# Converting float64 weights by a scaled copy and two bitwise VectorE operations

## The chip, the cores and the metric

The kernel runs on one core of a Trainium2 chip. The metric is the device time in microseconds (us), as the median of several runs; lower is better. TensorE (PE) does matrix products, VectorE (DVE), ScalarE (ACT) and GpSimd (POOL) do elementwise work, and SyncE (SP) issues most transfers.

## The reference, cut to what matters

```python
def reference(**kwargs):
    x = _attn_ref(q, k, v, mem_k, mem_v)          # chunked attention, 4 x 8 heads x 768 x 64
    x = x.transpose(0, 2, 1, 3).reshape(3072, 512)
    x = _moe_ref(x, w_gate, w1, w2)               # 8 experts, at most 384 tokens each
    return _moe2_ref(x, w1, w2, w3, w_out)        # (x@w1 * x@w2) @ w3 @ w_out

def _moe2_setup():
    n_tokens, d_model, d_ff = (3072, 512, 1024)
    return {'x': np.random.randn(n_tokens, d_model).astype(np.float32) * 0.3,
            'w1': np.random.randn(d_model, d_ff).astype(np.float32) * (1.0 / np.sqrt(d_model)),
            ...
```

The four weights of the last block arrive as float64: numpy promotes them when it multiplies by a float64 scalar. The kernel gets their raw bits, two 32-bit words for each number, and has to make float32 of them on the chip. Each is then split into a rounded high part and the rest (`hi`, `lo`), and products are made of three matmuls, so that they keep the accuracy of float32.

## The kernel before, in words

All instructions are written out by a planner in Python (`Plan.run`). Each piece of work is a generator that yields steps: engine letters ("P" TensorE, "V" VectorE, "A" ScalarE, "G" GpSimd, "D" a transfer), an estimated duration, the function that issues the instruction, and the time from which its inputs are there. The planner keeps a clock for each engine, takes the step that can start first, breaks ties by priority (a low number goes first), and so fixes the order of each engine's instructions. On the chip each engine works through its list in that order. A step marked "VG" goes to the one of VectorE and GpSimd that would end first, with 1.0 us (`BIAS`) added against VectorE.

The program has these stages, which overlap:

- Attention, up to about 97 us: 32 units (`unit`), each of score matmuls, softmax, transposes and value matmuls. TensorE, VectorE and ScalarE hand over to each other.
- Routing of expert 0 (`route(0)`), about 97 to 170 us: a search for a threshold, digit by digit. A digit is a compare over all tokens (L586, VectorE), counting matmuls (L651), a flag (L655), a summing matmul (L658) and small VectorE steps (L629, L644, L671). The stage ends with the tokens' indices (L773 to L791), then GpSimd gathers the tokens' rows (L829).
- In the same time `combine` multiplies w3 by w_out on TensorE (L503). It fills TensorE while the routing waits, and needs 24 converted tiles.
- The experts, from about 176 us: `first` (L489 to L491) and `second` over streamed weight blocks, `gate` (L927, L928, L935) with the 16 converted tiles of w1 and w2, `project` (L968, L969, L976), and the scatter. The routing of the next expert runs beside them. From about 246 us on the experts repeat.

The change touches `convert(n)`, which runs for 40 tiles of 128 x 512 numbers: n = 0 to 7 w_out (raw tiles `b`), n = 8 to 23 w3 (raw tiles `a`), n = 24 to 39 w1 and w2 (`a` and `b`). A tile needs two free places of 512 columns (`own`, `other`; mostly `cv`, also `x`). Its steps before:

- L448, ScalarE: the high word, read as float32, absolute value times 2^16, to `t`.
- L449, ScalarE: the top byte of the low word, to its top three bits as an integer, to `r`.
- L453 on GpSimd or L455 on VectorE: clamp, `t = max(t, 2.0)`.
- L458, VectorE: `t = (t << 3) | r`, bitwise, which gives the magnitude.
- n below 24 (`SIGNED`): L461, ScalarE, the sign of the high word to `r`; L462, GpSimd, `t = t * r`.
- n from 24: L465, VectorE: `t = (high & sign bit) | t`.
- L482, ScalarE: `hi`, the rounded copy. L399 on GpSimd or L401 on VectorE (`rest`): `lo = t - hi`.

The steps of `convert` have priority 70, those of a routing 50. L399 and L401 lie in the helper `rest`, which other stages use too.

Of the kernel before, what the change touches and what calls it, by code (L numbers as in the profile page):

```python
# [8 lines left out]
F32 = mybir.dt.float32  # L9
F32R = mybir.dt.float32r  # L10
BF16 = mybir.dt.bfloat16
I32 = mybir.dt.int32
U8 = mybir.dt.uint8
AF = mybir.ActivationFunctionType
OP = mybir.AluOpType
# [11 lines left out]
DM, DF, E = H * D, 1024, 8  # L27
CAP = N // E
NEG = -1.0e30
SIGNED = range(24)  # L30
STORE = 65
ABP = 61
ABN = 0
# [114 lines left out]
class Net:  # L148
# [289 lines left out]
    def convert(self, n):  # L438

        nc, V = self.nc, self.nc.vector  # L440
        t0 = yield from self.wait(("raw", n))
        places = [self.EARLY, self.CV] if n < 3 * FT else [self.CV]
        (own, tc, cv), (other, tr, r) = yield from Slots.pair(*places)
        tag, raw = self.raw.pop(n)
        t, ti = cv, cv.bitcast(I32)
        high = raw.rearrange("p (n w) -> p n w", w=2)[:, :, 1]
        byte = raw.bitcast(U8).rearrange("p (n w) -> p n w", w=8)[:, :, 3]
        e = yield ("A", 0.52, lambda: nc.scalar.activation(t, high.bitcast(F32), AF.Abs, scale=2.0 ** 16), max(t0, tc))  # L448
        er = yield ("A", 0.52, lambda: nc.scalar.activation(r.bitcast(I32), byte, AF.Copy, scale=1 / 32, bias=-31 / 64), max(t0, tr))  # L449

        def clamp(eng):
            if eng == "G":
                nc.gpsimd.tensor_scalar(t, t, 2.0, None, op0=OP.max)  # L453
            else:
                V.tensor_scalar(t, t, 2.0, None, op0=OP.max)  # L455

        e = yield ("VG", (0.34, 1.46), clamp, e)
        e = yield ("V", 0.60, lambda: V.scalar_tensor_tensor(  # L458
            ti, ti, 3, r.bitcast(I32), op0=OP.logical_shift_left, op1=OP.bitwise_or), max(e, er))
        if n in SIGNED:  # L460
            es = yield ("A", 0.52, lambda: nc.scalar.activation(r, high.bitcast(F32), AF.Sign), e)  # L461
            e = yield ("G", 1.23, lambda: nc.gpsimd.tensor_tensor(t, t, r, op=OP.mult), es)  # L462
            other.put(r, e)
        else:
            e = yield ("V", 0.60, lambda: V.scalar_tensor_tensor(  # L465
                ti, high, -2 ** 31, ti, op0=OP.bitwise_and, op1=OP.bitwise_or), e)
            other.put(r, e)
        self.at["read", n] = e
        if FT <= n < 3 * FT:
            m, i = divmod(n - FT, 2)  # L470
            if i == 0:
                ts, ws = yield from self.WS.get()
                self.wblk[m] = ts, ws, self.place(ws, [2, 2, 512], F32R)
            while m not in self.wblk:
                yield None
            ts, _, w = self.wblk[m]
            w = self.w[n] = w[:, i]
        else:
            ts, w = 0.0, self.place(tag, [2, 512], F32R)
            self.w[n] = w  # L480
        hi, lo = w[:, 0], w[:, 1]
        e = yield ("A", 0.52, lambda: nc.scalar.activation(hi, t, AF.Copy), max(e, ts))  # L482
        e = yield ("VG", (0.6, 1.23), lambda g: self.rest(hi, lo, t, g), e)
        own.put(cv, e)
        self.at["w", n] = e
# [622 lines left out]
```

## Time and profile before

| | |
|---|---|
| median of 3 runs | 923.13 us (922.63 to 924.12) |
| the profiled execution's own time | 923.5 us |
| its span in the trace | 921.7 us |
| mean granted TensorE clock | 0.983 of full speed |
| PE busy | 873.5 us (95%) |
| DVE busy | 613.2 us (67%) |
| ACT busy | 336.3 us (36%) |
| POOL busy | 203.4 us (22%) |

Busy times are those of the whole span. The stages differ much, so the rows further down are cut by stage. 1.8 us of the profiled execution's time lie outside its span.

### The profile page before, as it was taken

The numbers are of one execution on the slowest core, as the hardware profiler recorded it, in microseconds if no ns is written. First come the engines' busy times: TensorE is split into PE (matmuls) and PEld (weight loads), VectorE is DVE, ScalarE is ACT, GpSimd is POOL, SyncE is SP. The second block draws the span as 40 slices with busy tenths as digits, with TensorE's granted clock in tenths as the row PEclk, the third lists the DMA queues.
The fourth block names the chain that finished last, engine by engine and source line by source line (L and its number), as shares of the span: only waits on it lengthen the run. The fifth ranks groups of instructions, "written<-read, shape, count | busy, mean of one in ns | idle before, by whom it ended". The sixth has DMA issues, their size and how long they took to land.

```text
span 921.7 us, 16319 instructions
## 1 busy us (share of the span) xinstructions
PE 873.5 (95%) x6561; PEld 782.7 (85%) x6561; DVE 613.2 (67%) x1313; ACT 336.3 (36%) x593; POOL 203.4 (22%) x176
## 2 busy tenths in 40 slices
PE   6999877988998999999999999999999999999996
PEld 5777555887797998999899989979999999999995
DVE  7888799699875885789488767857764156213211
ACT  3778765466322331233223222321233134213211
POOL 3235677278642001101010101010110011001001
PEclk9999978997999999999999999999999999999999
DMA  8999880681061215025303601260141024002000
GB/s 298 403 343 390 302 292 7 215 309 55 16 186 44 80 69 154 35 70 134 88 35 114 174 3 57 94 175 1 55 152 46 1 81 162 10 1 103 1 1 34
DMA packets 36267, 110.36 MB, mean 120 GB/s; under 512 B 9440, under 2 KB 9952, under 8 KB 35552
## 3 DMA queue, kind: packets, MB, share of 16 engines
q1 hardware_dynamic: 32352, 96.74, 30.8%
q0 software_dynamic: 3840, 12.59, 4.3%
q8 instruction: 51, 0.84, 0.4%
q14 instruction: 24, 0.20, 0.1%
HBM read 96.24 MB, written 13.07 MB: 119 GB/s over the span
## 4 chain that ended last, share of the span: by engine, by line
PE 71%; DVE 17%; DMA 4%; issue 3%; ACT 2%; POOL 1%; SPq 0%; POOLq 0%; DVEq 0%; ACTq 0%
PE bank L927 9%; PE bank L935 9%; PE bank L928 8%; PE bank L489 7%; PE bank L490 7%; PE bank L491 7%; PE bank L976 5%; PE bank L968 5%; PE bank L969 4%; DVE kd L401 2%; PE bank L323 2%; DMA x<-xs,ix 2%; PE bank L340 2%; DVE ex L586 2%; PE bank L297 1%
## 5 line engine op out<-in xcount | busy, mean ns | idle before, releaser
L489 PE MATMUL bank<-x,kd 128*128 128x384 f32 x512 | 177.6, 347 | 0.1
L490 PE MATMUL bank<-x,kd 128*128 128x384 f32 x512 | 173.9, 340 | 1.3 <-DVE kd L401 1.3
L491 PE MATMUL bank<-x,kd 128*128 128x384 f32 x512 | 173.7, 339 | 0.0
L992 POOL DMA_INDIRECT out<-x,ix x24 | 23.4, 976 | 395.2 <-ACT x L987 392.2
L953 DVE TENSOR_TENSOR pt<-pt,bank 128x384 f32<-128x384 f32 x64 | 35.3, 552 | 111.5 <-PE bank L935 105.4
L490 PEld LDWEIGHTS bank<-x,kd 128*128 128x128 f32 x512 | 97.7, 191 | 3.0 <-DVE kd L401 2.3
L489 PEld LDWEIGHTS bank<-x,kd 128*128 128x128 f32 x512 | 97.7, 191 | 2.7 <-issue 1.6
L491 PEld LDWEIGHTS bank<-x,kd 128*128 128x128 f32 x512 | 97.4, 190 | 0.3 <-DVE x L401 0.3
L683 DVE TENSOR_SCALAR_CACHE_REDUCE ex<-cv,thf 128x1536 bf16<-128x1536 f32 x50 | 90.5, 1809 | 0.2
L927 PE MATMUL bank<-x,a 128*128 128x384 f32 x256 | 87.9, 343 | 0.0
L927 PE MATMUL bank<-x,b 128*128 128x384 f32 x256 | 87.4, 341 | 0.0
L928 PE MATMUL bank<-x,a 128*128 128x384 f32 x256 | 85.9, 335 | 0.0
L928 PE MATMUL bank<-x,b 128*128 128x384 f32 x256 | 85.7, 335 | 0.0
L946 ACT ACTIVATE pt<-bank 128x384 f32<-128x384 f32 x64 | 31.4, 491 | 143.3 <-PE bank L935 140.3
L957 ACT ACTIVATE x<-pt 128x384 fp32r<-128x384 f32 x64 | 33.5, 523 | 127.4 <-DVE pt L953 124.3
L968 PE MATMUL bank<-vd,x 128*128 128x512 f32 x192 | 77.0, 401 | 1.3 <-ACT x L957 1.3
L969 PE MATMUL bank<-vd,x 128*128 128x512 f32 x192 | 75.8, 395 | 0.0
L829 POOL DMA_INDIRECT x<-xs,ix x24 | 30.1, 1256 | 198.3 <-DVE ix L791 88.0
L976 PE MATMUL bank<-vd,x 128*128 128x512 f32 x192 | 66.8, 401 | 0.1
L890 ACT ACTIVATE x<-bank 128x384 fp32r<-128x384 f32 x64 | 31.3, 489 | 87.1 <-PE bank L491 79.3
L935 PE MATMUL bank<-x,a 128*128 128x384 f32 x256 | 56.6, 338 | 1.2 <-DVE x L401 1.1
L503 PE MATMUL bank<-b,kd 128*128 128x512 f32 x192 | 55.6, 440 | 0.6 <-DVE kd L401 0.4
(172 smaller groups left out, 1704.3 us busy)
## 6 DMA issues: line engine op xcount, KB each, us to landing
p<-in_w SPq DMA_DIRECT2D x32, 512.0 KB, 4.0
x<-in_w SPq DMA_DIRECT2D x32, 512.0 KB, 3.5
vd<-in_vw SPq DMA_DIRECT2D x32, 390.0 KB, 7.2
a<-in_w SPq DMA_DIRECT2D x16, 512.0 KB, 5.1
kd<-in_kT SPq DMA_DIRECT2D x32, 246.0 KB, 6.2
cv<-vs SPq DMA_DIRECT2D x5, 1536.0 KB, 13.0
a<-in_qT SPq DMA_DIRECT2D x16, 384.0 KB, 6.8
xs<-x SPq DMA_DIRECT2D x24, 256.0 KB, 4.8
```

The costliest lines, as they stand in the source:

```text
L489: mm(out, sh, mh, start=first, stop=False)
L490: mm(out, sl, mh, start=False, stop=False)
L491: mm(out, sh, ml, start=False, stop=last)
L503: t1 = yield ("P", DM * COL, lambda: self.nc.tensor.matmul(p, a, b, start=(kb + i == 0), stop=(kb == FT - 1 and i == 2)), max(t, t0))
L683: tv = yield ("V", 0.14 + m / 960, lambda: V.tensor_scalar(self.cb[:, :m], self.vt[:, m * i:m * i + m], ti.bitcast(F32), None, op0=OP.is_g ...
L927: mm(q, w[:, 0, 128 * c:128 * c + 128], self.yT[0][:, c], start=(c == 0), stop=False)
L928: mm(q, w[:, 1, 128 * c:128 * c + 128], self.yT[0][:, c], start=False, stop=False)
L935: mm(q, w[:, 0, 128 * c:128 * c + 128], self.yT[1][:, c], start=False, stop=(c == KT - 1))
L953: t = yield ("V", 0.47, lambda: nc.vector.tensor_tensor(self.gf, self.ta, p1[:, :CAP], op=OP.mult), max(t, t1))
L968: mm(p, g[:, 0, r], wc[:, 0], start=(m == 0), stop=False)
L969: mm(p, g[:, 0, r], wc[:, 1], start=False, stop=False)
L976: t = yield ("P", DM * COL, lambda: mm(p, g[:, 1, r], wc[:, 0], start=False, stop=(m == FT - 1)), t1)
```

## The change

The scale becomes 2^-112 in place of 2^16, and the copy keeps the sign. The shift by three then drops the sign and three upper bits of the exponent, which are now zero. No clamp is made. One bitwise VectorE operation picks the sign bit out of the scaled copy and merges it into the low bits `r`; a second shifts and merges. All 40 tiles take the same way. The planner's estimates change from 0.52 to 0.57 for the first two ScalarE steps and from 0.60 to 0.63 for the bitwise steps.

```diff
-SIGNED = range(24)
...
-        e = yield ("A", 0.52, lambda: nc.scalar.activation(t, high.bitcast(F32), AF.Abs, scale=2.0 ** 16), max(t0, tc))
-        er = yield ("A", 0.52, lambda: nc.scalar.activation(r.bitcast(I32), byte, AF.Copy, scale=1 / 32, bias=-31 / 64), max(t0, tr))
-
-        def clamp(eng):
-            if eng == "G":
-                nc.gpsimd.tensor_scalar(t, t, 2.0, None, op0=OP.max)
-            else:
-                V.tensor_scalar(t, t, 2.0, None, op0=OP.max)
-
-        e = yield ("VG", (0.34, 1.46), clamp, e)
-        e = yield ("V", 0.60, lambda: V.scalar_tensor_tensor(
-            ti, ti, 3, r.bitcast(I32), op0=OP.logical_shift_left, op1=OP.bitwise_or), max(e, er))
-        if n in SIGNED:
-            es = yield ("A", 0.52, lambda: nc.scalar.activation(r, high.bitcast(F32), AF.Sign), e)
-            e = yield ("G", 1.23, lambda: nc.gpsimd.tensor_tensor(t, t, r, op=OP.mult), es)
-            other.put(r, e)
-        else:
-            e = yield ("V", 0.60, lambda: V.scalar_tensor_tensor(
-                ti, high, -2 ** 31, ti, op0=OP.bitwise_and, op1=OP.bitwise_or), e)
-            other.put(r, e)
+        e = yield ("A", 0.57, lambda: nc.scalar.activation(t, high.bitcast(F32), AF.Copy, scale=2.0 ** -112), max(t0, tc))
+        er = yield ("A", 0.57, lambda: nc.scalar.activation(r.bitcast(I32), byte, AF.Copy, scale=1 / 32, bias=-31 / 64), max(t0, tr))
+        e = yield ("V", 0.63, lambda: V.scalar_tensor_tensor(
+            r.bitcast(I32), ti, -2 ** 31, r.bitcast(I32), op0=OP.bitwise_and, op1=OP.bitwise_or), max(e, er))
+        e = yield ("V", 0.63, lambda: V.scalar_tensor_tensor(
+            ti, ti, 3, r.bitcast(I32), op0=OP.logical_shift_left, op1=OP.bitwise_or), e)
+        other.put(r, e)
```

## Rows read from the trace of the kernel before

**Rows 1.** Busy us (instructions) of each engine by stretch; then clock, DMA share, GB/s

```profile
core 0: us, PE busy (x) PEld busy (x) DVE busy (x) ACT busy (x) POOL busy (x), PEclk, DMA share, GB/s
20.00:97.00 77.00, 73.09 (x1523) 54.08 (x1512) 63.66 (x197) 59.42 (x121) 29.91 (x22) 1.00 0.96 367
100.00:163.00 63.00, 49.26 (x310) 33.98 (x305) 57.57 (x103) 38.68 (x69) 47.41 (x31) 0.87 0.54 196
182.00:246.00 64.00, 55.31 (x396) 50.62 (x395) 62.53 (x98) 39.03 (x68) 49.90 (x28) 0.92 0.39 144
246.00:922.00 676.00, 660.57 (x3939) 615.10 (x3938) 401.48 (x866) 183.02 (x308) 62.09 (x75) 1.00 0.24 74
```

**Rows 2.** Longest wait of PE, 100 to 246 us: total us, times, longest

```profile
PE bank L651 <- DVE ex L586: 10.3, 7, 2.9
```

**Rows 3.** Chain of waits by line: 100 to 163, 182 to 246, 20 to 97

```profile
by line: issue 12.9%; PE bank L503 12.0%; DVE kd L401 9.8%; DVE ex L586 9.0%; DVE x L458 7.2%; DVE cv L455 7.0%; DVE cv L458 5.7%; DVE thr L629 4.2%; DVE vd L401 3.9%; ACT cv L461 2.5%; DVE B L644 2.2%; DVE e L727 2.2%; DVE e L577 1.9%; DVE
...
by line: DVE cv L465 14.7%; issue 13.6%; DVE kd L401 10.5%; DVE cv L458 10.2%; DVE ex L586 9.7%; DVE thr L629 3.9%; PE bank L489 3.9%; DVE x L891 3.9%; DVE x L401 3.4%; PE bank L491 2.8%; PE bank L490 2.8%; ACT cv L448 2.7%; DVE B L644 2.5%
...
by line: PE bank L323 21.9%; PE bank L340 18.5%; PE bank L297 17.1%; DVE small L308 8.1%; DMA b<-in_wo 8.0%; DVE ex L311 7.0%; PE bank L371 5.8%; DVE x L350 3.8%; issue 3.6%; PE bank L380 3.4%; DVE ex L586 1.7%; DVE cv L458 1.7%; DVE bank L
```

**Rows 4.** Instructions of single lines: ns shortest/median/longest, first and last start us

```profile
L458 DVE SCALAR_TENSOR_TENSOR cv<-cv x30: 648/681/1811, 22.0 to 241.8; 128x512 int32<-128x512 int32 x30
...
L455 DVE TENSOR_SCALAR cv<-cv x12: 389/427/1453, 21.3 to 226.9; 128x512 f32<-128x512 f32 x12
...
L629 DVE SCALAR_TENSOR_TENSOR thr<-tab,ki,B x8: 239/1088/1276, 120.9 to 238.6; 128x31 int32<-128x31 int32 x8
...
L644 DVE TENSOR_TENSOR B<-ki,B x8: 144/547/1277, 124.3 to 240.2; 128x1 int32<-128x1 int32 x8
...
L586 DVE TENSOR_TENSOR ex<-v,thr x15: 930/1732/2828, 113.1 to 604.5; 128x744 bf16<-128x744 f32 x8, 128x1512 bf16<-128x1512 f32 x7
...
L399 POOL TENSOR_TENSOR b<-cv,b x15: 1277/1300/2080, 25.8 to 244.2; 128x512 fp32r<-128x512 f32 x15
```

**Rows 5.** L458 alone, busy us (count) in both stretches

```profile
100.00:163.00 63.00, 13.29 (x15) 0.87 0.54 196
182.00:246.00 64.00, 13.72 (x16) 0.92 0.39 144
```

**Rows 6.** L465 alone, second stretch

```profile
182.00:246.00 64.00, 14.12 (x16) 0.92 0.39 144
```

**Rows 7.** L455 alone, both stretches

```profile
100.00:163.00 63.00, 7.74 (x11) 0.87 0.54 196
182.00:246.00 64.00, 2.52 (x3) 0.92 0.39 144
```

**Rows 8.** L401 alone, first stretch

```profile
100.00:163.00 63.00, 9.81 (x10) 0.87 0.54 196
```

**Rows 9.** L629 alone, sum of both stretches

```profile
sum 127.00, DVE 6.72; mean DVE 3.36
```

**Rows 10.** L644 alone, sum of both stretches

```profile
sum 127.00, DVE 5.02; mean DVE 2.51
```

**Rows 11.** L586 alone, sum of both stretches

```profile
sum 127.00, DVE 19.18; mean DVE 9.59
```

**Rows 12.** DVE timeline, L719 in route(0) and in route(1): start, us

```profile
154.74 1.21 DVE L719 TENSOR_SCALAR F<-cst,fm 128x8 f32<-128x8 f32 x1
...
248.02 0.23 DVE L719 TENSOR_SCALAR F<-cst,fm 128x8 f32<-128x8 f32 x1
```

**Rows 13.** L453 alone (clamp on POOL), both stretches

```profile
100.00:163.00 63.00, 6.25 (x4) 0.87 0.54 196
182.00:246.00 64.00, 26.85 (x13) 0.92 0.39 144
```

**Rows 14.** L462 alone (multiplication on POOL), first stretch

```profile
100.00:163.00 63.00, 25.52 (x16) 0.87 0.54 196
```

**Rows 15.** Chain of waits in order of time, behind the gather: start, us

```profile
178.06 1.64 PE bank L503 x7
```

**Rows 16.** A wait of the transfer queue, 100 to 160 us: total us, times, longest

```profile
SPq L436 <- ACT x L461: 11.5, 4, 4.5
```

## The prediction

> **What bounds the kernel now.** I read the busy times by stretch first. From 246 us on TensorE works 660.6 of 676 us, and no tile is converted there: the change can't move that part. All conversions lie before it, in three stretches [rows 1]: attention (20 to 97, TensorE 73.1 of 77 us), the first routing with the w3 tiles (100 to 163) and the first expert with the w1 and w2 tiles (182 to 246). In the last two TensorE has gaps, 63 - 49.3 = 13.7 and 64 - 55.3 = 8.7 us, while VectorE is busy 57.6 of 63 and 62.5 of 64. The mean granted clock is 0.87 and 0.92 of the 2.4 GHz level there and 1.00 in the other two stretches; what stands before the falls is TensorE idle. That loses about 0.13 x 63 + 0.08 x 64 = 13.3 us of TensorE's speed. So up to 22.4 + 13.3 = 35.7 us could come back if nothing else held TensorE up.
>
> Next the waits of TensorE between 100 and 246 us: the longest is the counting matmul that waits for a VectorE compare, 10.3 us in seven waits [rows 2]. The chain of waits says the same. In the two stretches its VectorE lines make 53% and 59%, with "issue", which here mostly sits inside stretched VectorE instructions, 66% and 72%; in attention the VectorE lines make only 22% [rows 3]. So VectorE's time sets the pace for about two thirds of the two stretches, and TensorE does in attention.
>
> Last, why is VectorE so slow there? The same instruction has very different durations [rows 4]: L458 has a median of 0.68 us and a longest of 1.81, the tiny L644 0.14 and 1.28, L629 0.24 and 1.28. The excess is at most 1.13 us and lies where GpSimd runs: L719 takes 1.21 us at 154.7, beside GpSimd's work, and 0.23 us at 248.0, where GpSimd is idle [rows 12]. I sum this excess over both stretches, duration minus the unhindered one [rows 4]:
> L458: 27.0 - 31 x 0.68 = 5.9 [rows 5]. L465: 14.1 - 16 x 0.68 = 3.2 [rows 6]. L455: 10.3 - 14 x 0.43 = 4.3 [rows 7]. L401, first stretch only, all of 512 columns like L458: 9.8 - 10 x 0.68 = 3.0 [rows 8]. L629: 6.7 - 8 x 0.24 = 4.8 [rows 9]. L644: 5.0 - 8 x 0.14 = 3.9 [rows 10]. L586: eight of 744 columns at 0.93, three of 1512 and one of 378 in proportion, 13.6 together; 19.2 - 13.6 = 5.6 [rows 11]. Six single instructions of the first routing like L719, about 0.98 each: 5.9 [rows 12].
> Sum 36.6 us. GpSimd ran 31 + 28 = 59 instructions in that time [rows 1], so one GpSimd instruction costs VectorE 36.6 / 59 = 0.62 us on average.
>
> **The change part by part.** *Clamps.* Fourteen of the two stretches' clamps are on VectorE, 14 x 0.43 = 6.0 us less [rows 4, 7]; 4 + 13 are on GpSimd [rows 13]. *Sign.* In the first stretch 16 GpSimd multiplications go [rows 14], and a second bitwise VectorE operation comes for each. It has two SBUF inputs of 512 int32 columns as L465 and L458 have, so 0.68 us unhindered and 1.81 at worst [rows 4]; I take 0.68 and count the hindrance apart: 16 x 0.68 = 10.9 us more. For n from 24 the operation only changes its operands: nothing. *Rests.* The other GpSimd instructions, 31 - 4 - 16 = 11 and 28 - 13 = 15, are rests (L399; one of them the expert's own). With GpSimd freed, the planner, which adds 1.0 us against VectorE, should put the 5 + 2 rests of tiles that are on VectorE there as well: 7 x 0.68 = 4.8 us less on VectorE, 7 instructions more on GpSimd. If it leaves them, the sum below changes by 0.5 us, so nothing hangs on it. VectorE's own work thus changes by 10.9 - 6.0 - 4.8 = +0.1 us.
>
> *Hindrance.* GpSimd keeps 59 - 33 + 7 = 33 instructions. At 0.62 us each VectorE loses 20.5 us to them instead of 36.6: -16.1. Bounds: the largest excess seen, 1.13, gives 37.3, which is 0.7 more than now. From below: with 33 instead of 59 instructions in the same time GpSimd's run back to back less often, so the mean could fall; I let it go to 0.5 (an estimate), 16.5 us, 20.1 less. I take 0.62, since it is a mean over both kinds of GpSimd instruction.
>
> The Trainium skill bears on this ("SBUF — State Buffer", section "SBUF: two separate sides"): VectorE and GpSimd share a pair of SBUF ports under an exclusive lock, which whoever starts first holds for the whole instruction, while the other is blocked; on VectorE's side it concerns instructions with two SBUF inputs and those in a two-port mode. The added operation is of that sort. By that rule each GpSimd instruction could cost VectorE its whole length; the rows' mean is half of that. The sum by the rule is the second rival's below.
>
> *ScalarE.* L461 goes; the first copy costs what the activation it replaces costs. ScalarE is busy 38.7 of 63 and 39.0 of 64 us [rows 1], so this hides beside VectorE: nothing; without that cover it would be a gain. *Transfers.* Loads of raw tiles wait 11.5 us for L461, the last reader of the raw tile [rows 16]; now L448 or L449 is the last. The tiles come earlier, but TensorE's long wait is for the compare [rows 2]: counted at nothing.
>
> *Attention.* Eight w_out tiles get a second bitwise operation, 8 x 0.68 = 5.4 us on VectorE, queued before softmax steps. VectorE has 13.3 us idle there and 22% of the chain: 0.22 x 5.4 = +1.2 us (bounds 0 and 5.4).
>
> *Sum.* VectorE: 0.1 - 16.1 = -16.0 us, of which the chain passes on two thirds [rows 3]: -10.7. With attention -10.7 + 1.2 = -9.5. From the profiled execution's 923.5 this gives 914.0; the median of the runs is 923.1, within their spread, so I leave it. All of it passed on, at 0.5 us and with attention free: 923.5 - 20.0 = 903.5. At 1.13 us: 0.1 + 0.7 = 0.8, two thirds are 0.5, plus 1.2: 925.2.
>
> **The rivals.** *The routing comes later.* The planner sees more work on VectorE and a new order. If one added operation stands ahead of the compare in each of the six digits, the gather comes 6 x 0.68 = 4.1 us later. TensorE has only seven matmuls of the combine left behind the gather, 1.64 us [rows 15], so 2.5 us would be lost and the first stretch would give nothing. The second still gives: edits -3 x 0.43 - 2 x 0.68 = -2.6, hindrance (28 - 17) x 0.62 = -6.8, two thirds of 9.4 = -6.3. Time 923.5 + 2.5 - 6.3 + 1.2 = 920.9. For it: TensorE's order is fixed, and the longest waits are already at the compare. Against: a routing's steps have the better priority.
>
> *Each GpSimd instruction that stays costs its whole length.* The place is both stretches: after the change VectorE runs little but two-input instructions around each tile, so each rest, 1.28 us unhindered [rows 4], may always find one to block: 33 x 1.28 = 42.2, VectorE +5.7, two thirds 3.8, time 923.5 + 3.8 + 1.2 = 928.5, slower. It decides above 1.05 us for each: (2/3)(0.1 + 33 x 1.05 - 36.6) + 1.2 = 0. For it: L629 has a median near its longest [rows 4]. Against: the mean of 0.62, and at least half of all L458 are unhindered. The Trainium skill's rule above ("SBUF — State Buffer") speaks for this rival, since the lock it describes is held for the whole instruction.
>
> *Hidden anyway.* TensorE's own work or the raw tiles' arrival takes over at once, and only attention's 1.2 us are left: 924.7. For it: the two stretches still hold 49.3 and 55.3 us of matmuls. Against: the 35.7 us of gaps and low clock.
>
> **How the numbers follow.** Forecast (914.0) 0.58; routing later (920.9) 0.18; hidden (924.7) 0.10; whole length (928.5) 0.14. A difference of 0.2%, about 1.8 us, is what a measurement of this kernel can tell. Faster: all of the forecast and 0.14 of the routing case, 0.72. Within it: 0.04 of the routing case and 0.06 of the hidden one, 0.10. Slower: 0.04 and 0.14, 0.18. The forecast's own range is 905 to 920. The whole range goes from 904, where all is passed on, to 925.5, which takes in the hidden case and the bound of 1.13 and leaves out the whole-length case and a little below.
>
> **What would show it.** No L453, L455, L461 and L462; two bitwise operations for each of 40 tiles, median 0.68. GpSimd near 33 instructions in the stretches between attention and the repeating experts. VectorE's excess near 20 us, and fewer instructions of L629 and L644 near 1.28. TensorE's wait at L651 under 10.3 us, its clock there nearer to 1.00, and the repeating experts starting some 10 us before 246. Attention ending about 1 us later. The prediction is wrong if the excess per GpSimd instruction rises above 1, if the gather does not come earlier, or if the repeating part itself changes length, for which I have no term.

## The result, and the profile after

The changed kernel takes 908.22 us, the median of four runs (907.21 to 908.99); the kernel before, run beside it, takes 922.88 us. The ratio is 0.9845, with a 95% interval of 0.9819 to 0.987. That is 14.7 us less, where 9.5 were forecast: the sign is right, the time lies in the range of 904 to 925.5, and the gain is half as large again as the sum made it. One run of the kernel before, beside the last experiment, took 4730.6 us and is left out of every comparison.

The profiled execution took 907.64 us. Its page, first the span, then the busy times:

```profile
span 905.9 us, 16251 instructions
...
PE 868.0 (96%) x6561; PEld 778.6 (86%) x6561; DVE 602.7 (67%) x1315; ACT 321.7 (36%) x569; POOL 138.0 (15%) x134
```

GpSimd has 138 us of work in place of 203, and VectorE, which got more instructions, 10.5 us less: 602.7 against 613.2. Its own work was to stay the same (+0.1 us in the two stretches, +5.4 in attention), so the difference is in how long the same instructions take. By stretch (columns as in [rows 1]; the bounds follow the stages, which now begin earlier, and the last row is the first stretch in the cut of before):

```profile
20.00:97.00 77.00, 72.32 (x1508) 53.24 (x1510) 64.59 (x198) 54.04 (x112) 10.27 (x8) 1.00 0.96 366
97.00:160.00 63.00, 53.68 (x402) 38.06 (x395) 56.95 (x119) 34.12 (x62) 25.49 (x15) 0.95 0.58 223
170.00:234.00 64.00, 57.69 (x416) 52.57 (x415) 62.35 (x104) 40.68 (x72) 29.81 (x17) 0.95 0.44 163
234.00:905.00 671.00, 659.82 (x3935) 614.40 (x3933) 399.42 (x859) 183.52 (x308) 61.38 (x75) 1.00 0.24 75
...
100.00:163.00 63.00, 54.48 (x383) 38.78 (x373) 55.94 (x116) 31.32 (x56) 26.24 (x16) 0.95 0.54 205
```

In the second and third row GpSimd has 15 + 17 = 32 instructions instead of 59, and VectorE is nearly as busy as before: it is still what the two stretches run by. From 100 to 163 us TensorE now executes 383 matmuls where it had 310, from 170 to 234 us 416 where it had 396 in the stretch that answers to it, and its granted clock is 0.95 in both, instead of 0.87 and 0.92.

Where in the run was the time won? Five milestones answer that best, since they don't depend on where a stretch is cut: the last value matmul (end of attention), the gather of expert 0, the first expert matmul, and the first and last gate matmul (the repeating experts lie between these two). Each row is one line of the code: ns shortest/median/longest, then first and last start in us. Before:

```profile
L340 PE MATMUL bank<-vd,pt x768: 271/273/299, 12.8 to 99.1; 128*32 128x130 f32 x192
...
L829 POOL DMA_INDIRECT x<-xs,ix x24: 946/1226/1946, 170.3 to 771.2; - x24
...
L489 PE MATMUL bank<-x,kd x512: 332/336/689, 179.5 to 862.7; 128*128 128x384 f32 x171
...
L927 PE MATMUL bank<-x,a x256: 333/334/443, 229.1 to 906.0; 128*128 128x384 f32 x128
```

After:

```profile
L339 PE MATMUL bank<-vd,pt x768: 271/273/299, 12.8 to 100.0; 128*32 128x130 f32 x192
...
L815 POOL DMA_INDIRECT x<-xs,ix x24: 946/1272/2265, 162.3 to 755.4; - x24
...
L475 PE MATMUL bank<-x,kd x512: 332/336/582, 170.5 to 846.8; 128*128 128x384 f32 x171
...
L913 PE MATMUL bank<-x,a x256: 333/334/443, 214.0 to 890.2; 128*128 128x384 f32 x128
```

| stage | before, us | after, us | difference |
|---|---|---|---|
| attention, to its last value matmul | 99.1 | 100.0 | +0.9 |
| from there to the gather | 71.2 | 62.3 | -8.9 |
| gather to first expert matmul | 9.2 | 8.2 | -1.0 |
| first expert matmul to first gate matmul | 49.6 | 43.5 | -6.1 |
| first to last gate matmul | 676.9 | 676.2 | -0.7 |

The gain lies in the two stretches that hold the conversions, 8.9 and 6.1 us, and attention pays 0.9. The repeating part keeps its length.

TensorE's wait for the compare is less than half of [rows 2]; after the change it is TensorE's longest from 97 to 234 us (total us, times, longest):

```profile
PE bank L637 <- DVE ex L572: 4.6, 4, 2.1
```

The two bitwise operations and the two small steps of a digit, as single lines:

```profile
L449 DVE SCALAR_TENSOR_TENSOR cv<-cv x31: 648/679/1581, 21.8 to 227.7; 128x512 int32<-128x512 int32 x31
...
L451 DVE SCALAR_TENSOR_TENSOR cv<-cv x31: 650/680/1708, 24.2 to 228.5; 128x512 int32<-128x512 int32 x31
...
L615 DVE SCALAR_TENSOR_TENSOR thr<-tab,ki,B x8: 232/238/1276, 118.2 to 224.1; 128x31 int32<-128x31 int32 x8
...
L630 DVE TENSOR_TENSOR B<-ki,B x8: 140/458/1239, 120.8 to 227.1; 128x1 int32<-128x1 int32 x8
```

The medians of the bitwise operations are the 0.68 us that the sum took. L615 (L629 before) has its median at 0.24 instead of 1.09: at least half of these are now unhindered. What remains looks like this; the timeline of VectorE, then a GpSimd instruction in the same stretch (start, us):

```profile
117.57 0.68 DVE L449 SCALAR_TENSOR_TENSOR cv<-x,cv 128x512 int32<-128x512 int32 x1
118.17 1.27 DVE L615 SCALAR_TENSOR_TENSOR thr<-tab,ki,B 128x31 int32<-128x31 int32 x1
119.36 0.68 DVE L451 SCALAR_TENSOR_TENSOR x<-x 128x512 int32<-128x512 int32 x1
...
117.87 1.51 POOL L398 TENSOR_TENSOR kd<-cv,kd 128x512 fp32r<-128x512 f32 x1 [10.35 <-ACT kd L468]
```

A rest starts on GpSimd at 117.87 and ends at 119.38; the 31-column step beside it, 0.23 us by itself, ends at 119.44. This is the excess of 1.04 us by one GpSimd instruction that [rows 4, 12] show as numbers. Summed over both stretches, VectorE's busy us on these two lines:

```profile
sum 127.00, DVE 26.04; mean DVE 13.02
...
sum 127.00, DVE 29.50; mean DVE 14.75
```

The merge (L449) has 26.0 - 32 x 0.68 = 4.2 us of excess, the shift (L451) 29.5 - 21.8 = 7.7, and, in the same way, L615 3.1, L630 3.5, the compare 0.7, single instructions of the routing 7.3. Together 26.5 us by 32 GpSimd instructions, 0.83 each. The prediction had 36.6 by 59 for the kernel before, 0.62 each; that sum is short by 2.8 us, as is told further down.

### The profile page after: what moved, and what is told of

It reads as the page before. It is cut to its first block, busy times and chain, and to the rows that moved or that the text cites. A ratio compares the mean times of both kernels' runs of the same rounds, so it can differ in the third digit from the quotient of the medians.

```text
span 905.9 us, 16251 instructions
## 1 busy us (share of the span) xinstructions
PE 868.0 (96%) x6561; PEld 778.6 (86%) x6561; DVE 602.7 (67%) x1315; ACT 321.7 (36%) x569; POOL 138.0 (15%) x134
## 4 chain that ended last, share of the span: by engine, by line
PE 69%; DVE 17%; DMA 7%; issue 4%; POOL 1%; ACT 1%; SPq 0%; POOLq 0%; ACTq 0%; DVEq 0%
PE bank L921 8%; PE bank L913 8%; PE bank L914 8%; PE bank L475 8%; PE bank L476 7%; PE bank L477 7%; PE bank L962 4%; PE bank L954 4%; PE bank L955 4%; DMA x<-xs,ix 3%; PE bank L339 2%; PE bank L322 2%; DVE cv L451 2%; DVE cv L449 1%; PE bank L296 1%
## 5 line engine op out<-in xcount | busy, mean ns | idle before, releaser
L913 PE MATMUL bank<-x,b 128*128 128x384 f32 x256 | 88.0, 344 | 0.0
L914 PE MATMUL bank<-x,b 128*128 128x384 f32 x256 | 86.2, 337 | 0.0
L921 PE MATMUL bank<-x,b 128*128 128x384 f32 x256 | 55.1, 336 | 0.0
## 6 DMA issues: line engine op xcount, KB each, us to landing
cv<-vs SPq DMA_DIRECT2D x5, 1536.0 KB, 12.8
```

What stands on the lines that cost most here:

```text
L913: mm(q, w[:, 0, 128 * c:128 * c + 128], self.yT[0][:, c], start=(c == 0), stop=False)
L914: mm(q, w[:, 1, 128 * c:128 * c + 128], self.yT[0][:, c], start=False, stop=False)
L921: mm(q, w[:, 0, 128 * c:128 * c + 128], self.yT[1][:, c], start=False, stop=(c == KT - 1))
```

## The experiments

Two theories were to be told apart. *Hindrance*: a GpSimd instruction that reads SBUF stretches VectorE's instructions, and the gain is the part of this that went away. *Chain*: the gain comes from the shorter way of a tile (no clamp, no activation, no GpSimd multiplication between ScalarE's copy and the rest), whoever does the work. A third question came up with the first results: the change alters the planner's estimates, so it also alters the order of everything around it.

**One half at a time.** The clamp alone is dropped:

```diff
-        e = yield ("A", 0.52, lambda: nc.scalar.activation(t, high.bitcast(F32), AF.Abs, scale=2.0 ** 16), max(t0, tc))
+        e = yield ("A", 0.52, lambda: nc.scalar.activation(t, high.bitcast(F32), AF.Abs, scale=2.0 ** -112), max(t0, tc))
...
-        e = yield ("VG", (0.34, 1.46), clamp, e)
```

> The kernel before with the clamp taken out alone: the first scale is 2^-112 with the absolute value, the sign is still multiplied in by GpSimd for n below 24. Hindrance theory (GpSimd instructions block VectorE): 17 GpSimd clamps fewer at 0.62 us are -10.5 us of hindrance, 14 VectorE clamps fewer are -6.0 us; two thirds of 16.5 passed on: 923 - 11 = about 912 us (908 to 916). Chain theory (each tile's chain of hand-overs is what got shorter, and the sign's path by ScalarE and GpSimd was the long part): less than half of the change's 15 us, 916 to 921.

Measured: 923.92 us, ratio 1.0004 [0.9981, 1.0028]. No gain. Or only the sign is merged bitwise for all tiles, and the clamp stays:

```diff
-SIGNED = range(24)
+SIGNED = range(0)
```

> The kernel before with all 40 tiles on the way of n from 24 (sign merged by a second bitwise VectorE operation); the clamps stay. Hindrance theory: VectorE +10.9 us in the first routing, 16 GpSimd multiplications fewer at 0.62 us are -9.9 us, attention +1.2: 922 to 926 us, no gain. Chain theory: one ScalarE and one GpSimd hand-over less per tile, raw tiles free earlier: 914 to 919.

Measured: 926.87 us, ratio 1.0046 [1.0019, 1.0073]. The chain theory's 914 to 919 is missed: a tile's way is shorter by an activation and a GpSimd multiplication, and the kernel is slower. Since the planner made a new order here too, this run alone doesn't decide. The groups of GpSimd's clamps between 97 and 246 us in this kernel (count | busy us, mean ns | idle before):

```profile
L453 POOL TENSOR_SCALAR cv<-cv 128x512 f32<-128x512 f32 x22 | 41.5, 1898 | 15.6 <-ACT cv L448 15.6
...
L453 POOL TENSOR_SCALAR x<-x 128x512 f32<-128x512 f32 x5 | 10.0, 2010 | 6.6 <-ACT x L448 6.6
```

There are 27 clamps on GpSimd now, where the same stretch of before has 18: the planner gave GpSimd, freed of 16 multiplications, nine clamps more. So 54 elementwise instructions are left there against 61 in the same stretch of before, and VectorE has 16 bitwise operations more to do.

The miss with the clamp (about 912 us expected) is another thing. GpSimd went from 61 to 47 instructions, VectorE from 133.9 to 122.4 busy us between 97 and 246 us, and nothing came of it. Its combine on TensorE and its gather:

```profile
L822 POOL DMA_INDIRECT x<-xs,ix x24: 946/1276/1947, 166.1 to 775.8; - x24
...
L496 PE MATMUL bank<-b,kd x192: 387/394/797, 104.0 to 182.9; 128*128 128x512 f32 x192
```

The gather is issued 4.2 us earlier than before, but TensorE works at the combine until 182.9 us, and the first expert's matmul starts at 183.1 instead of 179.5. So VectorE's saving was lost behind a new order of the work; the table at the end of this section shows it as VectorE's time without work. Whether the hindrance was worth what I thought could only be seen with the order held still.

**The order held still.** The next two kernels leave every step in the planner's reckoning, with its estimate, so that all other instructions stand where they stood, and only issue fewer. First no clamp at all is issued, on neither engine:

```diff
-                nc.gpsimd.tensor_scalar(t, t, 2.0, None, op0=OP.max)
...
-                V.tensor_scalar(t, t, 2.0, None, op0=OP.max)
+            pass
```

> The kernel before, with its planner still counting every clamp, so that the order of all other instructions stays as it was, but no clamp is issued (the first scale is 2^-112, which needs none). Taking the clamp out with a new order gave nothing (923.9 us); the order is the open point. Hindrance theory: the 14 VectorE and 17 GpSimd clamps of the two stretches are worth 6.0 + 10.5 us of VectorE time, two thirds passed on: 912 us (907 to 916). If the clamps cost nothing on the path, and order alone moves the time: 920 to 924.

Measured: 914.11 us, ratio 0.9896 [0.9862, 0.9931], 9.8 us less than before in the same series. Then VectorE's clamps are issued as before (with 0.0 as the bound) and only GpSimd's are not:

```diff
-            if eng == "G":
-                nc.gpsimd.tensor_scalar(t, t, 2.0, None, op0=OP.max)
-            else:
-                V.tensor_scalar(t, t, 2.0, None, op0=OP.max)
+            if eng == "V":
+                V.tensor_scalar(t, t, 0.0, None, op0=OP.max)
```

> As the run in which no clamp is issued, but VectorE's own clamps are issued (against 0.0, which changes nothing); only the 23 GpSimd clamps are gone, order as before. Hindrance theory: 17 x 0.62 = 10.5 us of VectorE time in the two stretches, two thirds: 916 us (911 to 919). If GpSimd's clamps cost nothing: 920 to 924, as before.

Measured: 918.61 us, ratio 0.9943 [0.9926, 0.9961], 5.3 us less. VectorE issues what it issued before, in the same order; only instructions of another engine are gone. A tile's way is shorter by the GpSimd clamp as well, but what shrank is VectorE's busy time: from the last value matmul to the first gate matmul 109.1 us instead of 116.3, with about as much time without work (14.6 and 13.7 us). So about half of the clamps' 9.8 us is GpSimd's hindrance. TensorE's wait for the compare, first with no clamp, then with VectorE's alone (97 to 245 us; 10.3 in [rows 2]):

```profile
PE bank L648 <- DVE ex L583: 7.6, 5, 2.7
```

```profile
PE bank L649 <- DVE ex L584: 8.7, 4, 3.3
```

**GpSimd work added back.** In the changed kernel GpSimd gets one addition more for each tile, over a scratch tile that nobody reads or waits for. The planner doesn't know of it, so the order stays:

```diff
+        self.idle = tile_("idle", [640], BF16)
...
+            x = self.idle[:, :512]
+            nc.gpsimd.tensor_tensor(x, x, x, op=OP.add)
```

> The changed kernel, order as it is, with one GpSimd addition over 512 columns of a scratch tile (two SBUF inputs, about 1.3 us) put in front of each tile's first bitwise step; nothing waits for it, it adds nothing to the result. Hindrance theory: 32 more GpSimd instructions in the two stretches at 0.62 to 0.8 us are 20 to 26 us of VectorE time, two thirds passed on: 908 + 13 to 17, so 921 to 926 us. Chain theory: GpSimd has room (it is busy 26 and 31 of 63 and 64 us), so 908 to 912.

Measured: 927.92 us, ratio 1.0047 [1.0026, 1.0067]. It is 19.7 us slower than the changed kernel, a little more than expected: the whole gain is gone and more. The added instructions between 97 and 245 us, and the gather:

```profile
L453 POOL TENSOR_TENSOR idle<-idle 128x512 bf16<-128x512 bf16 x30 | 42.7, 1423 | 1.1
...
L821 POOL DMA_INDIRECT x<-xs,ix x24: 946/1268/2253, 172.0 to 776.1; - x24
```

Thirty useless instructions in the stretches delay the gather from 162.3 to 172.0 us. The counterpart writes only: two memsets for each tile, so that GpSimd is busy longer still.

```diff
+            for _ in range(2):
+                nc.gpsimd.memset(self.idle, 0.0)
```

> As the run with an added GpSimd addition per tile (927.9 us), but with two GpSimd memsets of a scratch tile in its place: about as long on GpSimd, and no input is read. If it was the later rests behind them on GpSimd that cost the time: 920 to 930 again. If VectorE is hindered only by a GpSimd instruction that reads SBUF: 906 to 913, near the changed kernel.

Measured: 904.73 us, ratio 0.9791 [0.9758, 0.9825]. The memsets cost nothing, so it wasn't the rests' later turn on GpSimd either. Its timeline shows both cases within 4 us (start, us), the first two rows with a rest on GpSimd, the others beside four memsets:

```profile
126.76 1.28 POOL L400 TENSOR_TENSOR kd<-cv,kd 128x512 fp32r<-128x512 f32 x1
126.83 1.75 DVE L402 TENSOR_TENSOR kd<-x,kd 128x512 fp32r<-128x512 f32 x1
...
127.98 2.69 POOL L453 MEMSET idle<- 128x640 bf16 x4
129.20 0.67 DVE L454 SCALAR_TENSOR_TENSOR cv<-cv 128x512 int32<-128x512 int32 x1
129.87 0.67 DVE L457 SCALAR_TENSOR_TENSOR cv<-cv 128x512 int32<-128x512 int32 x1
130.47 0.23 DVE L621 SCALAR_TENSOR_TENSOR thr<-tab,ki,B 128x31 int32<-128x31 int32 x1
```

L402, 0.68 us by itself, takes 1.75 beside a rest; beside memsets the bitwise operations take 0.67 and the 31-column step 0.23. So it is not GpSimd's being busy that costs: additions, which read, cost 19.7 us, and memsets, which only write, nothing. Why this kernel is 3.5 us faster than the changed one is open; the two intervals of the ratio overlap (0.9819 to 0.987 and 0.9758 to 0.9825).

**Hardly any GpSimd work.** All rests of tiles from n = 8 go to VectorE:

```diff
-        e = yield ("VG", (0.6, 1.23), lambda g: self.rest(hi, lo, t, g), e)
+        e = yield ("VG" if n < FT else "V", (0.6, 1.23) if n < FT else (0.6,), lambda g: self.rest(hi, lo, t, g), e)
```

> The changed kernel with the rests of the tiles n from 8 on VectorE alone, so that GpSimd has nothing but gathers in the first routing and nearly nothing in the first expert. Hindrance theory, with 0.82 us for each as the changed kernel's trace has it: 31 x 0.68 = +21 us on VectorE, 31 x 0.82 = -25 us of hindrance: 908 - 3 = 905, with some 8 us either way for the new order (897 to 913). Without hindrance VectorE's added 21 us would show: 920 or more.

Measured: 908.14 us, ratio 0.9838 [0.9794, 0.9881], the same as the changed kernel. Its lines show what hindrance was left to win:

```profile
L451 DVE SCALAR_TENSOR_TENSOR cv<-cv x31: 650/681/692, 23.2 to 223.9; 128x512 int32<-128x512 int32 x31
...
L615 DVE SCALAR_TENSOR_TENSOR thr<-tab,ki,B x8: 232/244/247, 117.4 to 220.5; 128x31 int32<-128x31 int32 x8
...
L815 POOL DMA_INDIRECT x<-xs,ix x24: 947/1286/2257, 153.8 to 752.4; - x24
...
L913 PE MATMUL bank<-x,a x256: 333/334/443, 217.1 to 887.1; 128*128 128x384 f32 x128
```

The longest durations are now within 2% of the medians, and the gather comes at 153.8 us, 8.5 us earlier than in the changed kernel. But the first expert matmul then comes 13.5 us behind the gather instead of 8.2, and from there to the first gate matmul it takes 49.8 us (167.3 to 217.1) instead of 43.5. From the first to the last gate matmul it is 670.0 us instead of 676.2, for a reason that no run shows. In the end the 8.5 us became nothing. The same only for the w3 tiles, n = 8 to 23, where the stretch before the gather is won and the one behind it should stay as it was:

```diff
+        e = yield ("V" if FT <= n < 3 * FT else "VG", (0.6,) if FT <= n < 3 * FT else (0.6, 1.23), lambda g: self.rest(hi, lo, t, g), e)
```

> The changed kernel with the rests of the w3 tiles (n from 8 to 23) on VectorE alone; the others as in the changed kernel. With all rests on VectorE the gather came 8.5 us earlier, but the stage from the first expert matmul to the first gate matmul took 49.8 us, not 43.5. Hindrance theory: the first routing keeps that gain as far as the combine allows (3 us), and the second stretch keeps its 43.5 us: 905 (901 to 910).

Measured: 916.85 us, ratio 0.9925 [0.99, 0.995], a miss by 12 us. The gather is at 154.5, as meant, but the first gate matmul starts at 224.6 us, 10.6 later than in the changed kernel. What is won in one stage was given back in the next.

**The order by itself.** Three kernels issue the instructions of the changed one (one or two rests may change between VectorE and GpSimd) and differ only in the planner's estimates for the ScalarE and the bitwise steps (0.57 and 0.63 in the change). The cut shows the first of them:

```diff
-        e = yield ("A", 0.57, lambda: nc.scalar.activation(t, high.bitcast(F32), AF.Copy, scale=2.0 ** -112), max(t0, tc))
+        e = yield ("A", 0.52, lambda: nc.scalar.activation(t, high.bitcast(F32), AF.Copy, scale=2.0 ** -112), max(t0, tc))
...
-        e = yield ("V", 0.63, lambda: V.scalar_tensor_tensor(
+        e = yield ("V", 0.60, lambda: V.scalar_tensor_tensor(
```

> The changed kernel with the planner's old estimates (0.52 for the two ScalarE copies, 0.60 for the two bitwise steps); the instructions are the same, their order is not. Order theory (the gain comes from a luckier order): 914 us or more. Hindrance and chain theories: within 3 us of the changed kernel, 905 to 911.

> The changed kernel with one of its two new estimates taken back: 0.57 for the ScalarE copies stays, the bitwise steps are planned at 0.60. With both taken back it ran in 915.2 us. If the order effect is a systematic one of the estimates coming nearer to the chip (0.65 to 0.68 measured), this lies between, 909 to 914; if any small change of the estimates throws the order either way, it can lie anywhere from 903 to 918.

> The changed kernel with the bitwise steps planned at 0.75, between their unhindered 0.68 and their mean of 0.87 with hindrance. If better estimates give a better order: 908 or less. If the order is thrown by chance: anywhere from 903 to 918.

| ScalarE steps | bitwise steps | us | ratio to before |
|---|---|---|---|
| 0.57 | 0.63 (the change) | 908.22 | 0.9845 [0.9819, 0.987] |
| 0.52 | 0.60 | 915.16 | 0.9908 [0.9883, 0.9933] |
| 0.57 | 0.60 | 915.86 | 0.9915 [0.9885, 0.9945] |
| 0.57 | 0.75 | 918.87 | 0.9957 [0.9941, 0.9973] |

Nearly the same instructions take 908 to 919 us, by their order. The first of the three meets what the order theory asked for (914 or more) and misses what the hindrance and chain theories did (905 to 911): part of what the changed kernel gained can be its order. An estimate nearer to the hindered durations (0.75) isn't better. In the kernel with 0.52 and 0.60 a likely cause can be seen. The chain of waits shows the gathered rows' transfer, then TensorE's wait for it, then stretches of 5 us:

```profile
165.42 6.77 DMA x<-xs,ix
```

```profile
PE bank L831 <- DMA x<-xs,ix: 3.7, 1, 3.7
```

```profile
170.00:175.00 5.00, 2.76 (x12) 2.76 (x13) 2.76 (x4) 1.80 (x4) 0.00 (x0) 0.65 0.98 376
175.00:180.00 5.00, 5.00 (x21) 5.00 (x21) 3.62 (x7) 3.91 (x9) 0.00 (x0) 0.67 1.03 409
```

The transfer of the gathered rows takes 6.77 us on the chain, with the DMA engines at a share of 0.98 where it ends; TensorE is idle for 3.7 us and has a granted clock of 0.65 and 0.67 in these stretches. The gather itself was issued at 162.7, as in the changed kernel, where these rows land 3.4 to 4.1 us from their issue and TensorE doesn't wait for them at this place. The kernel with 0.75 has the same wait (5.4 us in three), the one with 0.57 and 0.60 hasn't. That the transfers collide is argued from this, not shown.

Last, the change in the old order: clamp, activation and GpSimd multiplication are counted by the planner and not issued, and the bitwise merge stands where the multiplication stood.

```diff
-                nc.gpsimd.tensor_scalar(t, t, 2.0, None, op0=OP.max)
...
-                V.tensor_scalar(t, t, 2.0, None, op0=OP.max)
+            pass
...
-            es = yield ("A", 0.52, lambda: nc.scalar.activation(r, high.bitcast(F32), AF.Sign), e)
-            e = yield ("G", 1.23, lambda: nc.gpsimd.tensor_tensor(t, t, r, op=OP.mult), es)
+            es = yield ("A", 0.52, lambda: None, e)
+            e = yield ("G", 1.23, lambda: V.scalar_tensor_tensor(
+                ti, high, -2 ** 31, ti, op0=OP.bitwise_and, op1=OP.bitwise_or), es)
```

> The instructions of the change (no clamp, sign merged by a bitwise VectorE operation for all tiles) in the order of the kernel before: the planner still counts clamps, sign activations and GpSimd multiplications with its old estimates, but none of them is issued; where the multiplication stood, the bitwise merge stands in VectorE's list. Hindrance theory with the prediction's own sum: 923 - 9.5 = 914 us (909 to 918), and what the changed kernel has below that is its new order. If the shorter chain of a tile is worth more by itself: 908 or less. If the bitwise operations cost what the multiplications did: 920 or more, less only the clamps' 9.8 us as measured (914).

Measured: 913.31 us, ratio 0.9859 [0.98, 0.9918]. Its two stretches:

```profile
97.00:160.00 63.00, 52.68 (x401) 37.42 (x402) 57.19 (x124) 35.77 (x65) 19.09 (x12) 0.97 0.62 230
...
173.00:237.00 64.00, 57.77 (x417) 53.05 (x417) 60.63 (x106) 40.37 (x71) 25.11 (x15) 0.95 0.40 150
```

These are nearly the changed kernel's own stretches: 401 and 417 matmuls against 402 and 416. The conversion alone, with nothing else moved, gives about what the prediction summed up for it: 10.3 us by the medians of its series (923.6 us before). The changed kernel's median lies 5 us lower, but the ratios (0.9859 and 0.9845) differ by 1.3 us only and their intervals overlap, so what the new order adds isn't shown by this pair.

**The runs side by side.** The stage from the last value matmul to the first gate matmul holds the conversions and, in every run, nearly the same matmuls. Before and after the change (columns as in [rows 1]):

```profile
99.10:229.10 130.00, 109.42 (x714) 87.81 (x703) 116.27 (x194) 76.52 (x132) 87.64 (x54) 0.89 0.55 196
...
100.00:214.00 114.00, 101.91 (x713) 82.35 (x703) 101.96 (x189) 65.30 (x115) 47.95 (x28) 0.96 0.59 221
```

The same stage in each run's profiled execution; the last column is the stage less VectorE's busy time:

| kernel | order | stage, us | VectorE busy | without work |
|---|---|---|---|---|
| before | its own | 130.0 | 116.3 | 13.7 |
| no clamp issued | of before | 119.4 | 104.1 | 15.3 |
| GpSimd's clamps not issued | of before | 123.7 | 109.1 | 14.6 |
| the change in the old order | of before | 115.2 | 102.4 | 12.8 |
| changed | its own | 114.0 | 102.0 | 12.0 |
| reads added | of changed | 129.1 | 118.0 | 11.1 |
| writes added | of changed | 111.8 | 98.9 | 12.9 |
| clamp alone dropped | new | 129.8 | 110.6 | 19.2 |
| sign alone merged | new | 131.7 | 114.1 | 17.6 |
| all rests on VectorE | new | 118.0 | 102.0 | 16.0 |
| w3 rests on VectorE | new | 124.8 | 110.2 | 14.6 |
| estimates 0.52, 0.60 | new | 123.3 | 104.7 | 18.6 |
| estimates 0.57, 0.60 | new | 120.7 | 101.7 | 19.0 |
| estimates 0.57, 0.75 | new | 117.8 | 99.6 | 18.2 |

Where the order is held, VectorE's time without work stays between 11.1 and 15.3 us, and the stage follows VectorE's busy time: of the four larger differences (the three kernels in the order of before, and the added reads) 0.87 to 1.06 arrives. A bad order shows in the last column: with other estimates VectorE has about as much work as in the changed kernel, or less, and 6 to 7 us more without any. In the kernel with 0.75 it isn't all: its way from the first to the last gate matmul takes 683.7 us instead of 676.2. These are single executions.

## Why the prediction was right, and where its sum was off

**The mechanism was right.** GpSimd's instructions stretch VectorE's; fewer of them speed up the two stretches. Taking away GpSimd's clamps and nothing else gave 5.3 us, adding thirty reads in the two stretches cost 19.7, adding writes cost nothing, and without GpSimd's rests no VectorE instruction of the two lines looked at is stretched. The rule of the Trainium skill that the prediction weighed ("SBUF — State Buffer", section "SBUF: two separate sides") confines this, for a VectorE instruction with two SBUF inputs, to GpSimd instructions that read SBUF. The runs agree, with 927.92 us for reads and 904.73 for writes.

**Terms that held.** Attention pays 0.9 us (1.2 taken). The bitwise operation costs 0.68. GpSimd keeps 32 instructions in the two stretches (33 counted), so the planner did move rests to it, six of the seven. TensorE's wait at the compare fell from 10.3 to 4.6 us, its clock rose to 0.95, and the gather came 8 us earlier. The repeating part kept its length (-0.7 us).

**Two terms were mis-sized.** The first is the price: "at 0.62 us each VectorE loses 20.5 us to them instead of 36.6". It loses 26.5, at 0.83 each. Two things stood behind the 0.62. The sum of before left out VectorE's rests of the second stretch, which have 1024 or 384 columns:

```profile
L401 DVE TENSOR_TENSOR x<-pt,x x57: 546/558/1633, 244.3 to 910.5; 128x384 fp32r<-128x384 f32 x57
L401 DVE TENSOR_TENSOR kd<-p,kd x32: 1199/1221/2252, 168.4 to 849.9; 128x1024 fp32r<-128x1024 f32 x32
```

Four of them lost 2.8 us there (the two longest are those of these lines), so it was 39.4 us by 59 instructions, 0.67 each. And the mean was taken over clamps, multiplications and rests together, while those that stay are nearly all rests. Clamps cost less: with GpSimd's clamps not issued, VectorE's busy time in the stage fell by 7.2 us for 14 GpSimd instructions, 0.51 each. (In the old order 27 instructions make about 20 us of excess in the two stretches, some 0.75 each, so the new order may have a part in the 0.83.) The lower bound, 0.5 for instructions that lie further apart, was argued in the wrong direction. In these stretches the hindrance thus fell by 12.9 us and not by 16.1.

The second term, and the one that matters more, is the share: "of which the chain passes on two thirds". With 12.9 the prediction's own arithmetic gives VectorE 0.1 - 12.9 = -12.8 us, two thirds of it -8.5, attention +0.9, so 923.5 - 7.6 = 915.9. Measured were 907.6 in that execution. The stage in the table, which ends at the same point of the program in both kernels, shows what is missing. VectorE's busy time fell by 14.3 us and the stage by 16.0: all of it was passed on, and 1.7 us of time without work went too. With attention's +0.9 and the repeating part's -0.7 that makes -15.8 of the 15.9 us. The runs with the order held pass on 0.87 to 1.06, so this is not the new order's doing. The chain's lines tell what came last at each step of the old run, and TensorE's own lines on it (12.0% for L503 in [rows 3]) didn't stay as they were: 713 matmuls took 101.9 us at a granted clock of 0.96, where 714 had taken 109.4 at 0.89. That the clock is why more than two thirds arrived is likely; no run isolates it.

One step the prediction lacked: it sized the instructions and left their order as it was. The change in the old order gave 10.3 us and the changed kernel 14.7; up to 5 us of that may be the order, which by the four variants is worth anything between 908 and 919 us. That the forecast came as near as it did owes something to luck, since the hindrance fell by less than it said and more of it arrived.

One reading was too general: "what stands before the falls is TensorE idle". Before four of the five falls of the clock in the two stretches TensorE was idle for 1.1 to 2.3 of 3 us, but from 116 to 119 us it was busy for 2.83 of 3 us at a granted clock of 1.00, and from 119 to 122 us the clock was 0.50. Nothing in the sum hangs on it.

**The rivals.** *Routing later*: no, the gather was issued at 162.3 instead of 170.3. *Hidden anyway*: no. In part it is seen, though: TensorE has 63 - 54.5 = 8.5 and 64 - 57.7 = 6.3 us of gaps left (13.7 and 8.7 before), and the longest piece in the chain of waits of the first stretch is now a transfer of a raw tile, not VectorE:

```profile
110.01 9.59 DMA a<-in_w
```

The prediction had counted these transfers at nothing, with the compare as the longer wait; that held while the compare was it. *Whole length for each GpSimd instruction*: no; its direction was right (0.83, not 0.62), its price of 1.28 was not reached, and neither was the 1.05 from which it decides.

**What stays open**: why the other orders leave VectorE more time without work; why the kernel with the clamp alone dropped kept its combine until 182.9 us; why the repeating part takes 670.0 us in one order and 683.7 in another; and why the kernel with memsets was the fastest (its VectorE is busy 3.1 us less in the stage). No version was found that clearly beats the changed kernel.

## What to carry to other kernels

A GpSimd instruction with a tensor read from SBUF, beside a stretch that VectorE sets the pace of, is not free: here each cost VectorE 0.5 to 0.8 us, and it shows as longer durations of VectorE's instructions, not as idle time. The share of an engine's lines in the chain of waits was too low a guess of what arrives: with the order held, 0.87 to 1.06 of VectorE's time did, not two thirds. Where a planner writes out the order, nearly the same instructions in another order moved this kernel by 11 us; so hold the order still (count the step, don't issue it) to learn what an instruction costs, and time several orders before one is believed to be better. What is won in one stage may be given back in the next, so compare milestones at the end of the stage that follows.

## What the runs showed of the hardware that was not expected

Memsets on GpSimd, 2.69 us for four of them, leave VectorE's two-input instructions beside them at 0.67 us, while rests of 1.28 us stretch them to 1.75. And VectorE's rests with one input in PSUM are not stretched even in the kernel before, in the same stretches in which L458 reaches 1.81 us. GpSimd works beside five of these eight; at 153.25 us one takes 0.68 us within a GpSimd rest of 1.74 us:

```profile
L401 DVE TENSOR_TENSOR vd<-bank,vd x8: 678/681/692, 115.9 to 180.3; 128x512 fp32r<-128x512 f32 x8
```

The hindrance seems to go both ways, though no run takes VectorE's instructions away to show it: rests on GpSimd, 1.28 us unhindered [rows 4], have a mean of up to 1.97 us in the changed kernel. Two groups of its GpSimd instructions from 97 to 234 us:

```profile
L398 POOL TENSOR_TENSOR b<-cv,b 128x512 fp32r<-128x512 f32 x8 | 15.6, 1947 | 11.9 <-ACT b L468 11.9
...
L398 POOL TENSOR_TENSOR kd<-x,kd 128x512 fp32r<-128x512 f32 x6 | 11.8, 1970 | 10.1 <-ACT kd L468 7.4 <-issue 2.6
```
